# A two-layer decode kernel on Trainium2: four V pages loaded in five parts each, with uneven rows

## The chip, the cores and the metric

The kernel runs on one core of one Trainium2 chip. The metric is device microseconds for one execution; a profiled execution gives the trace that the views come from, and its own time stands beside its span.

## What is computed

One token goes through two layers with the same weights. Each layer adds attention over a sliding window of cached keys and values, and then a gated feed-forward block, each behind a layer norm:

```python
D, Hq, Hkv, Sk, Dh = 640, 32, 32, 32768, 192
W = min(4096, max(256, Sk // 4))                  # 4096
q = (x @ wq).reshape(B, Sq, Hq, Dh).transpose(0, 2, 1, 3)
k, v = k_cache[:, :, Sk - W:, :], v_cache[:, :, Sk - W:, :]
scores = einsum("bhqd,bhkd->bhqk", q, k) * (Dh ** -0.5)
o = einsum("bhqk,bhkd->bhqd", softmax(scores), v)
A = o.transpose(0, 2, 1, 3).reshape(B, Sq, Hq * Dh) @ wo
B = (silu(x @ w1) * (x @ w3)) @ w2                # D to 1536 to D

x = x + A(layernorm(x));  x = x + B(layernorm(x))
x = x + A(layernorm(x));  x = x + B(layernorm(x))
```

Everything is bf16. A head's keys are 4096 x 192 values, 1.5 MB, and so are its values; 32 heads, two layers and the weights make some 220 MB that have to come from memory.

## The kernel before

**Pages.** A head's K or V in the window is a page: 128 partitions of 6144 values (12,288 bytes), row `p` holding 32 consecutive positions. An arena of 32 units (half a page each) holds pages and weights. Some K pages of layer 0 stay for layer 1 (`RETAIN`, line 34).

**The list of loads.** Before any work is issued, `loads` is filled for both layers in the order in which data will be wanted (lines 196 to 242): three pieces of wq; then for `i` from 0 to 37 the V page of head `i - 6` and the K page of head `i` (`LEAD` is 6; for the last four K pages the K page first); then wo and the feed-forward weights; then the same for layer 1. An entry is a key, a number of units and a list of parts; a part is an offset, a width and the source in memory. A page has one part.

**Issuing.** `refill` (line 258) takes loads from the front of the list as long as `place` finds room, and issues each part from SyncE (line 279). It is called at the start and by `done` (line 297) whenever a page has been used and its units come free. All these loads stand on SyncE's queue in the order of the list, so a load that has to wait holds up those behind it. Waits are put in by the framework: for the readers of what was in the units before, for the landing of an earlier load on the same completion counter, of which there are eight for SyncE's loads, and in the readers for the landing of each load that they read.

**Use.** `k_page` turns a K page on VectorE (line 401) and multiplies it with the query on TensorE into `s_ps`; `softmax_head` and `softmax_place` make the weights of four heads at a time; `v_page` (line 455) multiplies a V page with them into `o_ps`, sixteen matmuls of 128 x 384, each of which reads all 128 partitions. V of head `g` is used in the round of K of head `g + 6`. `wo_proj` and `ffn` follow, and their weights go through the same arena; layer 1 starts with ten half-page loads of wq.

The order of instructions on each engine is the order in which the program is written (`pin`).

Of the kernel before, what the change touches and what calls it, by code (L numbers as in the profile page):

```python
# [25 lines left out]
PGW = 6144  # L26
# [3 lines left out]
U = PGW // 2  # L30
# [8 lines left out]
MW = 2 * HB  # L39
PW = MW * HB  # L40
SPLIT = (("k", 12), ("v", 8), ("k", 13), ("v", 9), ("k", 15))
KW = 4 * HB
WH = 6 * KW + 32 - KW
KEEP = 2400
# [4 lines left out]
def _ap(t, p0, npart, off, dims):  # L49
    ps = t.ap[0][0]  # L50
    return bass.AP(t.tensor, t.offset + p0 * ps + off, [[ps, npart]] + [list(d) for d in dims])
# [3 lines left out]
def kernel(  # L55
# [13 lines left out]
    nc = tc.nc  # L69
# [12 lines left out]
    def pin(ins):  # L82
        tc.keep_in_program_order(ins)
        return ins

    def mm(*a, **k):
        return pin(nc.tensor.matmul(*a, **k))  # L87
# [58 lines left out]
    arena = arn.tile([P, NUNIT * U], BF16, name="arena")  # L146
# [7 lines left out]
    loads = []  # L154
# [9 lines left out]
    def head(layer, g):  # L164
        return HG * ORDER[layer][g // HG] + g % HG

    def k_head(layer, g):
        return HG * ORDER[1][0] + (0, 1, 2, 3, 6, 4, 5, 7)[g] if layer == 1 and g < HG else head(layer, g)

    def k_first(layer, i):  # L170
        return layer == 0 and H - HB <= i < H

    def wo_units(layer):
        if layer == 0:
            return [(("o", 0, 0), [(1, 0, 2880)]), (("o", 0, 1), [(1, 2880, 5760)]), (None, [(0, 0, 5120), (1, 6720, 7680)]),
                    (("o", 0, 2), [(1, 5760, 6720), (2, 0, 1920)]), (("o", 0, 3), [(2, 1920, 4800)]),
                    (("o", 0, 4), [(2, 4800, 7680)]), (("o", 0, 5), [(3, 0, 2880)]), (("o", 0, 6), [(3, 2880, 5760)]),
                    (("o", 0, 7), [(3, 5760, 7680)]), (None, [(0, 5120, 7680)])]
        return [(("o", 1, 0), [(0, 0, 7680)]), (("o", 1, 1), [(1, 0, 7680)]), (("o", 1, 2), [(2, 0, 6720)])]
# [4 lines left out]
    def q_pieces(layer):  # L184
        if layer == 0:
            at = (0, 12, 24, 60)
            return [tuple(range(a, b)) for a, b in zip(at, at[1:])]
        return [tuple(range(12 * c + 6 * f, 12 * c + 6 * f + 6)) for f in range(2) for c in range(NCH)]

    def tail_cuts(width):  # L190
        return (0, width - TAIL), (width - TAIL, 640), (width - 1280, 1280)

    def units_of(width):
        return -(-width // U)

    for layer in range(2):
        for piece in q_pieces(layer):
            n, at = 512 * len(piece), 512 * piece[0]
            loads.append((("q", layer, piece[0]), units_of(n), [(0, n, wq_r[:, at:at + n])]))
        for i in range(H + LEAD):  # L200
            kinds = (("v", i - LEAD, A_v_cache), ("k", i, A_k_cache))
            for kind, g, cache in kinds[::-1] if k_first(layer, i) else kinds:
                if not 0 <= g < H:
                    continue
                h = k_head(layer, g) if kind == "k" else head(layer, g)
                if kind == "k" and layer == 1 and h in RETAIN:
                    if h == STASH:
                        loads.append((("k", 1, h), 2, []))
                    continue
                src = cache[0, h, S0:SK, :].rearrange("(p t) d -> p (t d)", p=P)  # L210
                if layer == 1 and (kind, h) in SPLIT:
                    for th in range(2):
                        loads.append(((kind, layer, h, th), 1, [(0, U, src[:, U * th:U * th + U])]))
                else:
                    loads.append(((kind, layer, h), 2, [(0, PGW, src)]))
        for key, ranges in wo_units(layer):
            at, parts = 0, []
            for pos, lo, hi in ranges:
                parts.append((at, hi - lo, wo_v[ORDER[layer][pos]][:, lo:hi]))
                at += hi - lo  # L220
            if key:
                loads.append((key, units_of(at), parts))
            else:
                dst = wo5 if at == 2560 else wo4
                if dst is wo5:
                    src = parts[0][2]
                    parts = [(o, n, src[:, o:o + n]) for o, n in tail_cuts(2560)]
                loads.append((None, None if dst is wo5 else LAST, [(dst[:, o:o + n], src) for o, n, src in parts]))
        if layer == 0:
            loads.append((("fa", layer), 1, [(0, 3072, w1_v[:, 0:3072])]))  # L230
            loads.append((("fb", layer), 1, [(0, 3072, w1_v[:, 3072:6144])]))
            loads.append((("fc", layer), 1, [(0, 1536, w1_v[:, 6144:]), (1536, 1536, w3_v[:, 0:1536])]))
            loads.append((("fd", layer), 1, [(0, 3072, w3_v[:, 1536:4608])]))
            loads.append((("fe", layer), 1, [(0, 3072, w3_v[:, 4608:])]))
            loads.append((("fg", layer), 1, [(0, W2A, w2_v[:, 0:W2A])]))
            loads.append((("fh", layer), 1, [(0, 7680 - KEEP - W2A, w2_v[:, W2A:7680 - KEEP])]))
            loads.append((None, None, [(keep[:, o:o + n], w2_v[:, 7680 - KEEP + o:7680 - KEEP + o + n])
                                       for o, n in tail_cuts(KEEP)]))
        else:
            loads.append((("fa", layer), units_of(7680), [(0, 7680, w1_v[:, 0:7680])]))  # L240
            loads.append((("fb", layer), 2, [(0, 4608, w3_v[:, 0:4608])]))
            loads.append((("fc", layer), 1, [(0, 3072, w3_v[:, 4608:])]))
            loads.append((("fd", layer), 2, [(o, n, w2_v[:, o:o + n]) for o, n in ((0, 3200), (3200, 1280), (4480, 3200 - KEEP))]))

    def place(key, n):
        at = [s for s in free if all(s + i in free for i in range(n))]
        if n == 2:
            at = [s for s in at if s % 2 == 0] or at
        kind, layer, x = (key + (None,))[:3]
        if layer == 0 and kind == "k" and x in RETAIN and x != STASH:  # L250
            return min((s for s in at if s < LAST), default=None)
        if layer == 0 and kind == "o":
            at = [s for s in at if s < LAST]
        if n == 1:
            return min(at, key=lambda s: (s ^ 1) in free, default=None)
        return max(at, default=None)

    def refill():
        while loads:
            key, n, parts = loads[0]  # L260
            if key is None:
                if n is not None:
                    if n not in free or n + 1 not in free:
                        return
                    free.remove(n)
                    free.remove(n + 1)
                for dst, src in parts:
                    pin(nc.sync.dma_start(out=dst, in_=src))
                loads.pop(0)
                continue  # L270
            s = place(key, n)
            if s is None:
                return
            home[key] = list(range(s, s + n))
            for i in home[key]:
                free.remove(i)
            loads.pop(0)
            for off, w, src in parts:
                pin(nc.sync.dma_start(out=arena[:, s * U + off:s * U + off + w], in_=src))  # L279
            if not parts:  # L280
                stash(arena[:, s * U:s * U + PGW], False)

# [97 lines left out]
    def build_w(layer, b, first):  # L380
        engs = (nc.gpsimd, nc.scalar) + ((nc.vector, nc.vector) if first else (nc.gpsimd, nc.scalar))
        for a in range(4):
            dst = _ap(wst[:], 32 * a, 32, KW // 4 * a + HB - 1, [[WH - 1, HB], [KW, 6]])
            src = _ap(qt_sb[:], 0 if first else 32 * a, 32, 6 * HB * b, [[6, HB], [1, 6]])
# [18 lines left out]
    def k_page(layer, g, s_ps):  # L403
# [4 lines left out]
        for n in range(6):  # L408
            it = 5 - n
            be, par = divmod(it, 2)  # L410
            first = g % HB == 0 and n == 0
            w = 32 if first else KW
            for th in range(2):
                mm(s_ps[32 * th:32 * th + w, :], lhsT=wst[:, hl, KW * it:KW * it + w],
                   rhs=_ap(half(key, th), 0, P, 64 * be + par, [[192, 16], [2, 32]]),
# [7 lines left out]
    def softmax_head(b, s_ps):  # L423
# [7 lines left out]
        mb = _ap(m8[:], 0, 32, 0, [[0, 4], [1, HB]])  # L431
        pin(nc.vector.tensor_scalar_mul(out=tb[0:32, 0:KW].rearrange("p (a z) -> p a z", a=4), in0=mb, scalar1=-SCALE))
        pin(nc.scalar.mul(out=tb[32:64, 0:KW].rearrange("p (a z) -> p a z", a=4), in_=mb, mul=-SCALE))  # L433
        pin(nc.vector.transpose(nbt[:], tb[:]))  # L434
# [280 lines left out]
```

## Time and profile before

| | |
|---|---|
| median of 2 runs (526.09 and 526.28) | 526.18 us |
| the profiled execution, its own time | 526.2 us |
| its span, first to last instruction | 524.4 us |
| TensorE busy | 281.4 us (54%) |
| VectorE busy | 252.4 us (48%) |
| ScalarE and GpSimd busy | 68.4 and 19.3 us |
| loaded from memory | 219.74 MB, 419 GB/s over the span |
| a page from its issue to its landing, median | 29.2 us |

The page cuts the span into 40 slices of 13.1 us. Its DMA line is the mean busy share of the core's sixteen DMA engines in tenths, and the GB/s line is what they moved in each slice. A line of waits reads: engine and line that waited, for what, microseconds in total, times, longest. A line of a timeline or of the chain starts with the time from the span's start and the duration. "SPq" is SyncE's queue, which issues the loads; "PE" is TensorE, "DVE" VectorE, "ACT" ScalarE.

### The profile page before, as it was taken

How to read it: one execution, taken by the hardware profiler on the slowest of the kernel's cores; microseconds unless marked ns; L12 is line 12 of the kernel's file. 1: busy time of each engine (PE TensorE's matmuls, PEld its weight loads, DVE VectorE, ACT ScalarE, POOL GpSimd, SP SyncE). 2: the span in 40 equal slices, each digit the busy share in tenths (PEclk: the TensorE clock that was granted, in tenths of full speed). 3: DMA queues.
4: the chain of work that ended last, by engine and by line, in shares of the span. 5: the costliest groups of instructions: out<-in, count | busy, mean ns of one | idle time of the engine just before them, and what ended most of it. 6: DMA issues, size and time to landing. Idle time of an engine off the chain costs nothing.

```text
span 524.4 us, 6002 instructions
## 1 busy us (share of the span) xinstructions
PE 281.4 (54%) x2392; PEld 110.1 (21%) x2392; DVE 252.4 (48%) x369; ACT 68.4 (13%) x208; POOL 19.3 (4%) x88
## 2 busy tenths in 40 slices
PE   3325655462654544635555785574256564464565
PEld 1101221121222211212112232232113221121132
DVE  0079875556747476753001107431678565555101
ACT  1010220110202020202001022121201120112001
POOL 4000000000000000000000001000000000000100
PEclk9967776577666657666556579889666768577566
DMA  9999999999999999999999999999999999999995
GB/s 376 406 430 429 429 427 429 427 429 432 426 431 431 425 432 430 427 427 433 424 417 413 376 413 426 430 430 428 428 429 430 431 427 430 431 427 430 431 428 237
DMA packets 24083, 220.12 MB, mean 420 GB/s; under 512 B 2808, under 2 KB 3704, under 8 KB 8952
## 3 DMA queue, kind: packets, MB, share of 16 engines
q1 hardware_dynamic: 23912, 219.75, 99.2%
q8 instruction: 19, 0.31, 0.2%
q14 instruction: 8, 0.07, 0.0%
q10 hardware_dynamic: 144, 0.00, 0.0%
HBM read 219.74 MB, written 0.00 MB: 419 GB/s over the span
## 4 chain that ended last, share of the span: by engine, by line
DMA 89%; PE 7%; DVE 2%; ACT 1%; issue 0%; SPq 0%; DVEq 0%; ACTq 0%
DMA arena<-in_A_k_cache_dram 43%; DMA arena<-in_A_v_cache_dram 30%; DMA arena<-in_B_w_dram 7%; DMA arena<-in_A_wq_dram 6%; DMA arena<-in_A_wo_dram 3%; PE s_ps L87 2%; PE o_ps L87 2%; DVE arena L401 2%; PE y_ps L87 1%; PE pss L87 1%; PE q_ps L87 0%; PE u_ps L87 0%; PE g_ps L87 0%; ACT w L588 0%; SPq L279 0%
## 5 line engine op out<-in xcount | busy, mean ns | idle before, releaser
L87 PE MATMUL s_ps<-arena,wst 128*16 128x512 bf16 (+1 forms) x768 | 156.5, 524 | 158.5 <-DVE arena L401 85.4
L401 DVE STREAM_TRANSPOSE arena<-arena 128x1536 uint32<-128x1536 uint32 x100 | 171.3, 1754 | 74.7 <-DMA arena<-in_A_k_cache_dram 74.3
L87 PE MATMUL o_ps<-arena,ptm 128*8 128x384 bf16 (+1 forms) x1024 | 112.3, 428 | 29.1 <-DMA arena<-in_A_v_cache_dram 24.5
L87 PEld LDWEIGHTS <-wst 128*16 128x16 bf16 (+1 forms) x768 | 48.4, 108 | 248.1 <-issue 210.2
L87 PEld LDWEIGHTS <-ptm 128*8 128x8 bf16 (+1 forms) x1032 | 41.2, 100 | 70.9 <-issue 57.3
L433 ACT ACTIVATE nt<-m 32x16 f32<-32x16 f32 x16 | 3.4, 213 | 272.2 <-DVE m L430 272.2
L449 ACT COPY ptm<-w 32x64 bf16<-32x64 bf16 x80 | 23.6, 295 | 45.4 <-PE o_ps L87 43.3
L87 PE MATMUL q_ps<-arena,xs 128*32 128x512 bf16 x120 | 19.2, 583 | 13.1 <-DMA arena<-in_A_wq_dram 12.0
L478 DVE SCALAR_TENSOR_TENSOR w<-pss,sc,cb 64x192 bf16<-64x192 f32 x16 | 6.5, 409 | 40.9 <-PE pss L87 40.9
L385 POOL COPY wst<-qt_sb 32x24 bf16<-32x24 bf16 x30 | 8.4, 279 | 421.9 <-PE s_ps L87 307.7
L424 DVE TENSOR_REDUCE lt<-s_ps 64x1 f32<-64x512 f32 x16 | 10.9, 684 | 24.4 <-PE s_ps L87 24.0
L87 PE MATMUL y_ps<-arena,otd 128*1 128x320 bf16 x176 | 15.3, 437 | 10.2 <-DMA arena<-in_A_wo_dram 9.8
L439 DVE STREAM_TRANSPOSE w<-w 64x512 bf16<-64x512 bf16 x16 | 11.3, 705 | 14.4 <-ACT w L436 14.4
L327 DVE CAST w<-y_ps 128x320 bf16<-128x320 f32 x3 | 1.5, 492 | 28.5 <-PE y_ps L87 28.5
L87 PEld LDWEIGHTS <-xs 128*32 128x32 bf16 x200 | 7.6, 112 | 31.7 <-issue 27.4
L449 DVE COPY ptm<-w 32x64 bf16<-32x64 bf16 x48 | 10.0, 209 | 8.8 <-PE o_ps L87 7.7
L385 DVE COPY wst<-qt_sb 32x24 bf16<-32x24 bf16 x4 | 1.1, 275 | 25.9 <-ACT qt_sb L372 25.8
L472 ACT CAST w<-o_ps 128x384 bf16<-128x384 f32 x16 | 7.7, 478 | 32.4 <-PE o_ps L87 25.1
L436 ACT ACTIVATE w<-s_ps,nt 64x512 bf16<-64x512 f32 x16 | 10.9, 682 | 5.6 <-DVE nt L434 5.6
L87 PE MATMUL pss<-w,sel 128*64 128x192 bf16 x32 | 6.2, 281 | 8.3 <-ACT w L472 6.9
L87 PEld LDWEIGHTS <-otd 128*1 128x1 bf16 x186 | 5.7, 102 | 19.9 <-issue 15.5
L87 PE MATMUL pss<-xsq,sc 128*128 128x6 f32 x16 | 4.7, 369 | 8.3 <-ACT xsq L104 7.5
(84 smaller groups left out, 117.0 us busy)
## 6 DMA issues: line engine op xcount, KB each, us to landing
arena<-in_A_v_cache_dram SPq DMA_DIRECT2D x62, 1536.0 KB, 29.2
arena<-in_A_k_cache_dram SPq DMA_DIRECT2D x47, 1536.0 KB, 29.2
arena<-in_A_wq_dram SPq DMA_DIRECT2D x10, 768.0 KB, 7.4
arena<-in_A_wq_dram SPq DMA_DIRECT2D x1, 4608.0 KB, 20.0
arena<-in_A_k_cache_dram SPq DMA_DIRECT2D x6, 768.0 KB, 10.6
arena<-in_A_wo_dram SPq DMA_DIRECT2D x6, 720.0 KB, 8.7
arena<-in_B_w_dram SPq DMA_DIRECT2D x5, 768.0 KB, 8.5
arena<-in_A_wo_dram SPq DMA_DIRECT2D x2, 1920.0 KB, 30.0
```

Of the source, the lines that this page charges most:

```text
L87: return pin(nc.tensor.matmul(*a, **k))
L327: pin(nc.vector.tensor_copy(out=y_sb[:, 320:640], in_=y_ps[1][:, 0:320]))
L385: pin((engs[a].copy if engs[a] is nc.scalar else engs[a].tensor_copy)(out=dst, in_=src))
L401: pin(nc.vector.transpose(x, x))
L424: pin(nc.vector.reduce_max(out=t0[:, 0:1], in_=s_ps[0:64, :], axis=AX.X))
L433: pin(nc.scalar.mul(out=tb[32:64, 0:KW].rearrange("p (a z) -> p a z", a=4), in_=mb, mul=-SCALE))
L436: pin(nc.scalar.activation(out=e[:], in_=s_ps[0:64, :], func=ACTF.Exp, bias=nbt[:, 0:1], scale=SCALE, accum_out=l[0:64, b % 2:b % 2 + 1]))
L439: pin(nc.vector.transpose(et[:], e[:]))
L449: pin((eng.copy if eng is nc.scalar else eng.tensor_copy)(out=dst, in_=src))
L472: pin(nc.scalar.copy(out=o_sb[:, 0:384], in_=o_ps[:, 0:384]))
L478: pin(nc.vector.scalar_tensor_tensor(out=om, in0=ot_ps, scalar=rl[0:64, b % 2:b % 2 + 1], in1=mask[0:64].unsqueeze(2).broadcast_to([64, 16 ...
```

## The change

Four V pages of layer 0 are loaded in five parts. They are the pages at places 1, 6, 11 and 16 of the V order, and `UNEVEN` gives each a number `k`: 8, 12, 14 and 10. The parts, all with the full 12,288 bytes of each row:

- 64 rows: partitions 0, 2, 4, ...
- 32 rows: partitions 1, 5, 9, ...
- 16 rows: partitions 3, 11, 19, ...
- `k` rows: partitions 7, 15, 23, ... (every eighth)
- `16 - k` rows: the rest of every eighth partition, from `7 + 8 k` on

A part carries a function that picks its rows, and `refill` applies it to the destination and the source. Offsets in the arena, order of the list, users and everything else stay.

```diff
+UNEVEN = {1: 8, 6: 12, 11: 14, 16: 10}
...
+    def uneven(src, k):
+        if k is None:
+            return [(0, PGW, src)]
+
+        def take(first, step, n):
+            def rows(x):
+                ps = x.ap[0][0]
+                return bass.AP(x.tensor, x.offset + first * ps, [[step * ps, n], list(x.ap[1])])
+            return rows
+
+        picks = ((0, 2, 64), (1, 4, 32), (3, 8, 16), (7, 8, k), (7 + 8 * k, 8, 16 - k))
+        return [(0, PGW, src, take(*pick)) for pick in picks]
...
-                    loads.append(((kind, layer, h), 2, [(0, PGW, src)]))
+                    loads.append(((kind, layer, h), 2, uneven(src, UNEVEN.get(g) if layer == 0 and kind == "v" else None)))
...
-            for off, w, src in parts:
-                pin(nc.sync.dma_start(out=arena[:, s * U + off:s * U + off + w], in_=src))
+            for off, w, src, *rows in parts:
+                dst = arena[:, s * U + off:s * U + off + w]
+                if rows:
+                    dst, src = rows[0](dst), rows[0](src)
+                pin(nc.sync.dma_start(out=dst, in_=src))
```

## The prediction

> **What bounds the kernel now.** I read the page first: the line of the DMA share, the bytes per second, the queues, the chain that ended last.
>
> ```profile
> span 524.4 us, 6002 instructions
> ...
> PEclk9967776577666657666556579889666768577566
> DMA  9999999999999999999999999999999999999995
> GB/s 376 406 430 429 429 427 429 427 429 432 426 431 431 425 432 430 427 427 433 424 417 413 376 413 426 430 430 428 428 429 430 431 427 430 431 427 430 431 428 237
> ...
> q1 hardware_dynamic: 23912, 219.75, 99.2%
> q8 instruction: 19, 0.31, 0.2%
> ...
> DMA 89%; PE 7%; DVE 2%; ACT 1%; issue 0%; SPq 0%; DVEq 0%; ACTq 0%
> ```
>
> The sixteen DMA engines are busy from the first slice to the last but one, at about 430 GB/s, and 89% of the chain is transfers. 219.75 MB at 430 GB/s are 511 us of the 524.4. So only what slows the engines, idles them, or makes the slowest of them later can move the time. The one dip is at the border of the layers: slices 20 to 24 (424, 417, 413, 376, 413) lie 107 GB/s in all under 430, which is 107 / 430 x 13.11 us = 3.3 us of lost transfer.
>
> Then what SyncE, which issues every load, waits for:
>
> ```profile
> SPq L279 <- DMA arena<-in_A_v_cache_dram: 196.0, 60, 7.3
> SPq L279 <- DMA arena<-in_A_k_cache_dram: 135.9, 43, 3.8
> SPq L619 <- DVE w L617: 22.3, 1, 22.3
> SPq L279 <- PE o_ps L87: 20.9, 18, 3.6
> ```
>
> and its timeline early in layer 0, around the first V page that the change splits (the 25.26 line; the others are issued at 63.29, 99.80 and 136.43):
>
> ```profile
> 21.63 0.33 SPq L279 DMA_DIRECT2D arena<-in_A_k_cache_dram  x1
> 25.26 0.33 SPq L279 DMA_DIRECT2D arena<-in_A_v_cache_dram  x1
> 28.90 0.33 SPq L279 DMA_DIRECT2D arena<-in_A_k_cache_dram  x1
> ```
>
> A page is 1.57 MB, 3.66 us at 430 GB/s, and one is issued every 3.64 us; it lands 29.2 us later (the median of the page's DMA issues). 29.2 / 3.65 = 8: SyncE keeps eight loads in flight and issues the next when the oldest has landed. That is what its 332 us of waiting on landings are.
>
> Last, the chain at the border of the layers:
>
> ```profile
> 288.40 1.60 PE y_ps L87 x11
> 290.00 0.02 issue
> 290.02 6.91 DMA arena<-in_A_wq_dram
> 296.93 0.04 issue
> 296.97 1.05 PE q_ps L87 x5
> 298.02 0.02 issue
> 298.04 6.53 DMA arena<-in_A_wq_dram
> 304.57 0.04 issue
> ```
>
> Here loads wait for buffers that PE frees, and PE for loads that have landed. So a load counts here when its slowest engine has landed it. The trace records sixteen completions a load, one an engine (without the engine's number), and I read how far the last lags the first. For the K page that lands from 42.89 to 43.45 us it is 0.56 us. At 44.08 us one engine carries an instruction packet of 16 KB (0.96 us; the q8 line), and the next load's last completion lags 2.13 us, the others 0.57 as before. Such packets come some 30 us apart, each makes one engine about 1.5 us later, and it stays late. The w2 load that lands at 286.75 to 289.79 has seven completions within 0.45 us, eight from 1.11 to 1.47, and one at 3.04. By the load that completes the chain at 304.57 the lag is 1.26: the earlier engines have idled meanwhile. At the kernel's last weight load it is 3.20 us again (mean 1.3).
>
> **The change, part by part.** The sum is against the profiled execution: 526.2 us, of which 524.4 are span and 1.8 lie around it; the median of the runs is 526.18, so no shift between them.
>
> Sixteen more issues on SyncE. Each takes 0.328 us (the rows of line 279), 5.2 us in all, beside 332 us of waits for landings: hidden, cost 0. Behind a waiting part stand all later loads, for SyncE issues in order. Five of the eight loads in flight now make up one page, so the store shrinks from eight pages to the three after it plus what is left of the split one: 3.5 pages or more, 12.8 us. That cover would have to fall to the time from issue to landing with nothing in front, 1.0 to 1.6 us for the store of the output at the end, before engines idle. The parts land within one page time, five full pages are issued after them, and the next split page is ten loads later. Cost 0.
>
> Packets. The rows stay 12,288 bytes. The packet records show one engine's rows starting 456.5 ns apart and the 4-byte packet that closes a load taking 6 ns (8 x 456.5 + 6 = 3,658 ns a page). Four more closing packets a page, four pages: 16 x 6 = 0.1 us on every engine, on the path. Cost +0.1 us.
>
> PE. The first matmul of a split page must see five landings in place of one: 16 more waits at some 0.017 us (SyncE's EVENT_SEMAPHORE row), 0.3 us. Behind them queue that page's sixteen matmuls and the next K page's. PE is busy 54% and in the stretch from 20 to 160 us waits for K transposes (33.0 us), never for V pages: hidden. Without that cover it would be the 0.3 us.
>
> Rows an engine carries. 64, 32 and 16 rows can be shared as 4, 2 and 1 by sixteen engines; k and 16 - k rows cannot be shared evenly. One engine can get none, one or two of them: 7 to 9 rows a page for 8 now, and 4 rows more or fewer in the four pages, 4 x 456.5 = 1.83 us. The total stays. How loads of fewer than 128 rows are dealt out, no row shows, for before has none. What it is worth is set at the border: if the latest engine there (3.04) is relieved, the next at 1.47 becomes the last, a gain of at most 1.57 us; if it gets four rows more, a loss of 1.83. After the border the lags start afresh, and the shift is carried to the end. The trace does not say which engines are the late ones, so between -1.57 and +1.83 I take 0.
>
> [...]
>
> Where the rows are written. A full page runs at 456.5 ns a row on every engine whether they are in step (0.56 us) or 2 us apart, so in a full page no engine is in another's way. For rows on every second, fourth or eighth partition the bounds are: nothing, as in the full pages, the nearest rows; and above, each row taking double because two engines share a way into the memory, 4 x 3.66 = 14.6 us. I take nothing, since rows and packets are the same size as now.
>
> Sum: 526.2 + 0 + 0.1 + 0 + 0 + 0 = **526.3 us**.
>
> **Rivals.**
>
> Relief. The late engines are those that get fewer rows. For it: the lag at 289.79 is one engine's, and 1.57 us of it are there to be had; the 3.3 us lost at the border are mostly this. Against: four page times with no regard to which engine is hit later. 526.3 - 1.57 = 524.7 us.
>
> Burden. The same with the other sign: the engine at 3.04 gets rows. 526.3 + 1.83 = 528.1 us.
>
> Engines in each other's way (the other side). If the rows of a part are dealt out in runs, the write ways that one engine had to itself in a full page are shared by two, while others lie idle. The price is up to one page time a page: 526.3 + 14.6 = 540.9 us when all engines are in step. They are in step to 0.56 us when the first split page comes and one to six of them are 1 to 2 us off later, which softens it: half is 533.6. It decides for slower by 2% (10.5 us) from 72% of the doubling on. Against it: 430 GB/s whatever the lags, in full pages.
>
> [...]
>
> Parts that wait for one another. If a part had to wait for the landing of the one before it, the eight loads would run dry sixteen times, at some 2 us each: about 558 us. The partitions of the parts are disjoint, so I give it little.
>
> Nothing moves: if the engine goes by the partition that is written, every engine keeps 8 rows, and the time is the forecast's.
>
> **How the numbers follow.** Forecast (nothing moves, or what moves does not meet the late engines; 525.7 to 527): 0.32. Relief: 0.27. Burden: 0.13. Engines in each other's way: 0.25, of which 0.11 are above 536.7. Waiting parts: 0.02. Faster by over 2%, which would take nearly all of the 13 us that the span lies above 511: 0.01. A measurement of this kernel tells about 2% from no change. Within 2%: 0.32 + 0.27 + 0.13 + 0.14 = 0.86; slower 0.11 + 0.02 = 0.13; faster 0.01. Range: 524.5 to 535.0 leaves 0.03 below and 0.17 above. Without the contention the time lies in 524.5 to 528.5.
>
> **What would show it.** SyncE's issues of line 279 rise by 16 with 0.33 us each, and 29.2 us stays the median landing. The GB/s of the slices around 55, 93, 130 and 167 us stay at 425 to 430 (a dip to 215 to 350 there is the third rival; dips to nothing are the waiting parts). The spread of the completions after 170 us tells relief, burden or nothing: 1.8 us in before. The chain at the border shows whether its landings at 296.93 and 304.57 come earlier or later. Wrong would be a loss outside these places, above all idle PE time in front of V pages.

## The result and the profile after

| | before | after |
|---|---|---|
| median | 526.18 us (526.09 to 526.28, 2 runs) | 570.92 us (570.32 to 571.52, 2 runs) |
| profiled execution, its own time | 526.2 us | 571.5 us |
| its span | 524.4 us | 569.4 us |

The ratio is 1.085 (95% interval 1.08 to 1.09): 44.7 us slower. The prediction was 526.3 us, with 524.5 to 535.0 as its range. Medians here and below are of runs in the usual, faster state; one run below, of e15_arena_runs, was in a slower one and is left aside.

First the page of the changed kernel; a slice is now 14.2 us. Line numbers of `k_turn` and `refill` have moved: 401 is now 418, and 279 is 296.

```profile
span 569.4 us, 6030 instructions
...
DMA  9999994599399489999899999999999999999996
GB/s 380 407 428 387 429 428 194 226 428 429 108 401 429 193 339 429 382 431 422 329 405 419 394 409 375 411 431 429 426 428 431 428 431 429 431 428 429 430 431 270
...
DMA 66%; PE 15%; DVE 9%; issue 6%; ACT 1%; SPq 1%; POOL 1%; DVEq 0%; POOLq 0%; ACTq 0%
```

The chain that ended last was 89% transfers and is now 66%; what has grown in it is PE (7% to 15%), VectorE (2% to 9%) and issue (0% to 6%). The GB/s line has three holes, near 85 to 114 us (194, 226), 142 to 157 (108) and 185 to 214 (193, 339). Taking each slice's lack against 430 GB/s times 14.2 us, the whole line lacks 57.5 us of transfer; the line of before lacks 12.4 us in the same way. The difference, 45.1 us, is the whole of the longer span. The three holes (to 171 us for the second) hold 14.6 + 11.7 + 10.8 = 37.1 us of it, the slice of 387 1.4, and the stretch from 270 to 370 us, around the layers' border, 8.9, where the border of before lacks 3.3.

Three stretches inside the holes, with the busy time of PE, PE's weight load, VectorE, ScalarE and GpSimd (their instructions in brackets), the clock, the DMA share and GB/s:

```profile
91.00:107.00 16.00, 4.62 (x20) 1.39 (x22) 10.50 (x13) 2.77 (x9) 0.55 (x2) 0.61 0.34 121
132.00:152.00 20.00, 3.21 (x12) 0.83 (x12) 4.06 (x5) 0.48 (x1) 0.00 (x0) 0.50 0.59 238
191.00:206.00 15.00, 6.38 (x56) 2.81 (x56) 11.53 (x12) 0.07 (x1) 0.56 (x2) 0.66 0.33 120
```

The DMA engines are idle for two thirds of the first and the third. So they are not slow here: nothing has been issued to them. The reason stands in VectorE's waits. The one row with a V page in it:

```profile
DVE arena L418 <- DMA arena<-in_A_v_cache_dram: 92.6, 4, 26.6
```

Line 418 is the transpose of K pages. It waits four times for a V page, 92.6 us in all, and there was no such row before. VectorE's timeline shows the four places (start, duration, and in the brackets the idle time ahead and its releaser):

```profile
57.16 3.44 DVE L418 STREAM_TRANSPOSE arena<-arena 128x1536 uint32<-128x1536 uint32 x2 [26.63 <-DMA arena<-in_A_v_cache_dram]
...
95.28 6.76 DVE L418 STREAM_TRANSPOSE arena<-arena 128x1536 uint32<-128x1536 uint32 x4 [23.83 <-DMA arena<-in_A_v_cache_dram]
...
145.89 3.44 DVE L418 STREAM_TRANSPOSE arena<-arena 128x1536 uint32<-128x1536 uint32 x2 [22.24 <-DMA arena<-in_A_v_cache_dram]
...
194.29 10.07 DVE L418 STREAM_TRANSPOSE arena<-arena 128x1536 uint32<-128x1536 uint32 x6 [19.94 <-DMA arena<-in_A_v_cache_dram]
```

In before the first of these transposes runs as soon as the query is ready:

```profile
29.70 3.44 DVE L401 STREAM_TRANSPOSE arena<-arena 128x1536 uint32<-128x1536 uint32 x2
```

The waits that the trace records with each instruction agree with that. The first K transpose of before waits on one landing counter. In the changed kernel it waits on five, those of the five parts of the V page at place 1, which it does not read; the transposes at 95.28, 145.89 and 194.29 us, which follow the issue of the pages at places 6, 11 and 16, wait on five, four and five, and so do the first K matmuls behind each. These waits are put in by the framework, which, by these waits, takes the two to overlap.

Now SyncE's timeline around the second split page (start, duration):

```profile
73.05 6.31 SPq L296 DMA_DIRECT2D arena<-in_A_v_cache_dram  x5
101.53 0.34 SPq L296 DMA_DIRECT2D arena<-in_A_k_cache_dram  x1
```

After the fifth part, at 79.4 us, SyncE issues nothing for 22 us. The next load needs units that K pages hold; their transposes wait for the V page just issued, so everything in flight has to land first, then VectorE and PE have to free a page. SyncE's waits name both, where before named mostly landings (196.0 and 135.9 us, and 20.9 for `o_ps`):

```profile
SPq L296 <- PE o_ps L88: 94.3, 35, 10.7
...
SPq L296 <- DVE arena L418: 70.0, 15, 19.4
SPq L296 <- PE s_ps L88: 51.0, 22, 6.4
```

### The profile page after: what moved, and what is told of

Read it like the earlier page. It is cut to its first block, busy times and chain, and to the rows that moved or that the text cites. A ratio compares the mean times of both kernels' runs of the same rounds, so it can differ in the third digit from the quotient of the medians.

```text
span 569.4 us, 6030 instructions
## 1 busy us (share of the span) xinstructions
PE 269.2 (47%) x2392; PEld 108.1 (19%) x2392; DVE 250.9 (44%) x369; ACT 68.3 (12%) x208; POOL 19.3 (3%) x88
## 4 chain that ended last, share of the span: by engine, by line
DMA 66%; PE 15%; DVE 9%; issue 6%; ACT 1%; SPq 1%; POOL 1%; DVEq 0%; POOLq 0%; ACTq 0%
DMA arena<-in_A_v_cache_dram 32%; DMA arena<-in_A_k_cache_dram 18%; PE s_ps L88 10%; DMA arena<-in_A_wo_dram 8%; DVE arena L418 7%; DMA arena<-in_B_w_dram 5%; PE o_ps L88 3%; DMA arena<-in_A_wq_dram 2%; SPq L296 1%; PE pss L88 1%; ACT ptm L466 1%; PE q_ps L88 1%; PE y_ps L88 1%; POOL wst L402 1%; DVE otd L499 0%
## 5 line engine op out<-in xcount | busy, mean ns | idle before, releaser
L88 PE MATMUL s_ps<-arena,wst 128*16 128x512 bf16 (+1 forms) x768 | 150.0, 503 | 224.3 <-DVE arena L418 162.6
L418 DVE STREAM_TRANSPOSE arena<-arena 128x1536 uint32<-128x1536 uint32 x100 | 170.0, 1748 | 124.8 <-DMA arena<-in_A_v_cache_dram 92.6
L88 PE MATMUL o_ps<-arena,ptm 128*8 128x384 bf16 (+1 forms) x1024 | 109.5, 413 | 15.6 <-DMA arena<-in_A_v_cache_dram 15.5
L402 ACT COPY wst<-qt_sb 32x24 bf16<-32x24 bf16 x30 | 8.7, 290 | 0.7
```

The costliest lines, as they stand in the source:

```text
L402: pin((engs[a].copy if engs[a] is nc.scalar else engs[a].tensor_copy)(out=dst, in_=src))
L418: pin(nc.vector.transpose(x, x))
```

## Experiments

The theory: the waits of the K transposes cost nearly all. The rival: the write side of the parts costs it (the prediction's third rival), and the waits only show where the time is lost. All kernels ran beside runs of before on the same chip.

| kernel | median, us (runs) | before there | ratio, 95% interval |
|---|---|---|---|
| e1_wait_only | 565.95 (2) | 525.6 | 1.077, 1.0741 to 1.0799 |
| e2_own_split | 534.05 (4) | 525.6 | 1.0169, 1.0142 to 1.0195 |
| e3_own_whole | 525.66 (10) | 525.6 | 1.0002, 0.9993 to 1.0012 |
| e4_own_even | 533.75 (4) | 525.6 | 1.0157, 1.014 to 1.0174 |
| e5_own_halves | 526.05 (10) | 525.97 | 1.0002, 0.9993 to 1.0012 |
| e6_src_plain | 533.29 (4) | 525.97 | 1.014, 1.0124 to 1.0155 |
| e7_dst_plain | 553.53 (4) | 525.97 | 1.0512, 1.048 to 1.0544 |
| e8_two_halves | 565.57 (2) | 525.97 | 1.0756, 1.0731 to 1.0781 |
| e10_page1 | 526.99 (10) | 525.85 | 1.003, 1.0019 to 1.0041 |
| e11_page6 | 538.89 (4) | 525.85 | 1.0254, 1.0237 to 1.0271 |
| e12_wait_late | 525.61 (10) | 525.85 | 1.0005, 0.9994 to 1.0016 |
| e13_thirtytwos | 525.62 (10) | 525.85 | 0.9999, 0.999 to 1.0009 |
| e14_half_ways | 543.2 (4) | 525.69 | 1.0314, 1.025 to 1.0377 |
| e15_arena_runs | 555.46 (3) | 525.69 | 1.0553, 1.0523 to 1.0583 |

### The wait alone, and the split alone

**e1_wait_only**: the kernel before, with the wait put in by hand.

```diff
+    OWN = [("v", 0, head(0, g)) for g in (1, 6, 11, 16)]
+    seen = []
...
+            if key in OWN:
+                seen.append(key)
             for off, w, src in parts:
...
         turned.add(key)
+        while seen:
+            pin(nc.vector.tensor_copy(out=pad[0:1, 0:1], in_=page(seen.pop())[0:1, 0:1]))
```

> The kernel before, its four V pages whole, and four VectorE copies of one element more: each reads one of the V pages 1, 6, 11 and 16, just before the K transposes that wait for the split pages in the changed kernel. Theory W (the time is lost because K transposes wait for V pages that are issued long before they are used): 560 to 575 us, with VectorE starting its first K transposes at 55 to 58 us instead of 29.7. Rival S (the time is lost in the split loads themselves, their rows or their number): 526 to 528 us, since here no load is split and four tiny copies cost under 0.5 us.

Measured: 565.95 us, 40.4 above before. Its page and its row of waits:

```profile
DMA  8999994799399399999899999999999999999996
GB/s 363 422 430 431 427 430 182 270 430 417 136 405 429 151 404 426 390 429 416 324 423 420 395 412 408 423 434 427 429 428 431 427 430 428 431 428 429 431 430 267
```

```profile
DVE pad L405 <- DMA arena<-in_A_v_cache_dram: 88.6, 4, 24.9
```

The pages are whole here, and the three holes are there all the same, in the same slices. The wait alone makes 40 of the 45 us.

**e2_own_split**: the change, but the four V pages go, one after the other, into a tile of their own (two units, taken from the arena), so that nothing else in the arena can be taken for them.

```diff
+    side = arn.tile([P, 2 * U], BF16, name="side")
-    arena = arn.tile([P, NUNIT * U], BF16, name="arena")
+    arena = arn.tile([P, (NUNIT - 2) * U], BF16, name="arena")
+
+    def span(s, off, w):
+        return side[:, s * U + off:s * U + off + w] if s < 2 else arena[:, (s - 2) * U + off:(s - 2) * U + off + w]
...
+        if key in OWN:
+            OWN.remove(key) if 0 in at and n == 2 else None
+            return 0 if 0 in at else None
+        if OWN:
+            at = [s for s in at if s >= 2]
...
-                dst = arena[:, s * U + off:s * U + off + w]
+                dst = span(s, off, w)
```

> The split of the changed kernel, part for part, but the four V pages go to a tile of their own (two units taken out of the arena), so that no K transpose and no K matmul waits for them. Theory W: most of the 44.7 us go; what stays is the stretched rows that the changed kernel's trace shows (12,288-byte packets of up to 900 to 1,100 ns for some 3 us around each split page, 1.3 to 2.3 us a page), so 531 to 536 us. Rival S: 560 us or more.

Measured: 534.05 us, 8.4 above before (7.5 to 10.2 by the interval). VectorE waits for no V page any more, and the engines never idle; but the slices of the split pages are thinner:

```profile
DMA  9999999999999999999999999999999999999995
GB/s 370 414 429 427 380 428 404 387 428 384 396 430 380 410 429 429 429 429 422 409 416 395 419 417 424 430 429 428 429 430 429 430 429 427 429 430 429 430 428 246
```

So there is a second, smaller cost, and it is one of busy engines. 40.4 + 8.4 are 48.8, 4 more than the change costs; some of the stretched transfer falls into time in which the engines would have run dry anyway. That last reading is inferred.

**e3_own_whole**: the same tile, with whole pages.

```diff
-UNEVEN = {1: 8, 6: 12, 11: 14, 16: 10}
+UNEVEN = {}
```

> As the run with the split pages in a tile of their own, but these pages come whole again, one load each: what the tile of its own costs by itself. Both theories: 526 to 527.5 us.

Measured: 525.66 us, no difference. The tile of its own costs nothing, so e2's 8.4 us are the split's.

**e4_own_even**: e2 with even parts.

```diff
-        picks = ((0, 2, 64), (1, 4, 32), (3, 8, 16), (7, 8, k), (7 + 8 * k, 8, 16 - k))
+        picks = ((0, 2, 64), (1, 4, 32), (3, 8, 16), (7, 8, 16))
```

> The tile of its own, with four parts of 64, 32, 16 and 16 rows: the same partitions, and no engine gets more rows than another. If uneven rows by themselves matter (an engine that gets up to four rows more or fewer), this lies 1 to 2 us off the run with k and 16 - k rows, to either side; if only the stretched rows of small parts matter, both agree within 1 us, at 531 to 536 us. Rival S in the form of too many parts: a fifth less of the loss than with five parts.

Measured: 533.75 us, against 534.05 with uneven parts, well within both intervals. That the rows are uneven, the subject of Relief, Burden and Nothing moves, costs nothing that can be measured.

### When the wait costs

**e8_two_halves**: the change in the arena, with two halves a page in place of five parts. Its parts are those of e5_own_halves (below), which has them in a tile of their own.

```diff
-        picks = ((0, 2, 64), (1, 4, 32), (3, 8, 16), (7, 8, k), (7 + 8 * k, 8, 16 - k))
+        picks = ((0, 2, 64), (1, 2, 64))
```

> The changed kernel with two parts in place of five, 64 rows on even and 64 on odd partitions, in the arena: no uneven rows and no small parts, but the same waits of K transposes and K matmuls for these pages. Theory W: 563 to 569 us, as the run that adds the wait alone to whole pages. Rival (small or uneven parts make the loss): 526 to 530 us.

Measured: 565.57 us, against 526.05 for the same loads in a tile of their own: 39.5 us. The row of waits:

```profile
DVE arena L418 <- DMA arena<-in_A_v_cache_dram: 87.3, 4, 25.5
```

Here the parts themselves cost nothing, and the wait costs its 40 us. It needs neither five parts nor uneven ones.

**e10_page1** and **e11_page6**: the change with one split page.

```diff
-UNEVEN = {1: 8, 6: 12, 11: 14, 16: 10}
+UNEVEN = {1: 8}
```

```diff
-UNEVEN = {1: 8, 6: 12, 11: 14, 16: 10}
+UNEVEN = {6: 12}
```

> The changed kernel with only the first of its four V pages split (k = 8); the other three come whole. Theory: the K transposes on VectorE and the K matmuls that follow the issue of a split page wait for all its parts to land. For the page at place 1 that puts the first transpose some 24 us later (29.7 to about 54 us), but the arena is filled far ahead, and eight loads are in flight; SyncE runs out of free units only some 27 us after the start of the stall, so the engines idle for a few us at most: 526 + 2 (stretch of the parts) + 0 to 3 = 528 to 531 us, and the GB/s stay above 380 in the slices after the first. Rival (each of the four waits costs alike, a quarter of the 44.7 us): 537 us, with a slice near 200 GB/s within 30 us after 54 us.

> The changed kernel with only the page at place 6 split (k = 12). Theory: compute runs close behind the loads at that time, so its stall of some 24 us leaves SyncE without free units for about 22 us and the engines idle for about 11.5 us (from the 16 us at 121 GB/s of the changed kernel's trace), 2 us of stretched parts besides, and a page or two of thinner transfer behind: 538 to 542 us; no idle time of VectorE in front of a K transpose at 54 us, one of 20 to 25 us near 95. Rival (a quarter of the loss for each page): 537, which the time alone does not tell from the theory; the trace does, for by the rival the GB/s would fall at once when the page is issued, and by the theory only some 20 us later.

Measured: 526.99 and 538.89 us, 1.1 and 13.0 above before. First page 1, VectorE's wait and the GB/s:

```profile
DVE arena L418 <- DMA arena<-in_A_v_cache_dram: 27.1, 1, 27.1
```

```profile
GB/s 373 408 432 427 383 426 429 430 430 426 432 430 425 432 432 423 431 430 429 427 408 416 412 420 426 432 428 426 431 430 428 430 429 429 431 428 430 429 426 234
```

VectorE stands still for 27.1 us, and the engines do not notice: only the slice of the split page itself is thin (383, 1.4 us). The expectation's 528 to 531 was too high: it allowed 2 us for the stretch and up to 3 for idling. SyncE still has free units to fill until 56.5 us, and the loads in flight by then last over the 8 us in which it waits for the next (to 64.8 us). Then page 6, VectorE's timeline and the GB/s:

```profile
92.80 6.75 DVE L418 STREAM_TRANSPOSE arena<-arena 128x1536 uint32<-128x1536 uint32 x4 [48.38 <-DMA arena<-in_A_v_cache_dram]
```

```profile
GB/s 367 418 428 428 432 429 313 124 417 429 426 429 430 428 430 430 427 431 427 429 420 420 412 423 425 433 423 431 431 426 430 430 427 431 430 425 433 427 430 225
```

The time is as expected, the stall is not: 48.4 us in place of 20 to 25, since without page 1's stall VectorE comes to the waiting transpose at 44.4 us, before the V page is even issued (63.2 us). The loss is no longer for it. The slices of 313 and 124 lack 13.2 us, and SyncE issues nothing from 78.4 to 99.0 us. So the length of VectorE's stall does not set the cost. What does is for how long the next load on SyncE needs units that are freed behind the stall: 8 us in e10, some 21 here.

**e12_wait_late**: the four one-element reads of e1, put where each page is used.

```diff
+                if layer == 0 and g in (1, 6, 11, 16):
+                    pin(nc.vector.tensor_copy(out=pad[0:1, 0:1], in_=page(("v", layer, head(layer, g)))[0:1, 0:1]))
                 v_page(layer, g, o_ps[b])
```

> The kernel before, all pages whole, and four one-element copies on VectorE that read the V pages at places 1, 6, 11 and 16, as in e1_wait_only, but each put in front of the sixteen matmuls that use the page, a page's turn after its load was issued six K pages earlier in the list. The copies write a scratch element that nothing uses, so nothing of the result is changed. Theory: what costs 40 us in e1_wait_only is that VectorE waits for a page that was issued up to the arena's whole depth ahead of the work; here the page has landed before the K page that VectorE turns next or lands just ahead of it, so 526 to 527 us and no wait for a V page above 4 us in VectorE's waits. Rival (a wait on a V page costs as such, or the four copies do): 535 us or more.

Measured: 525.61 us, no difference, and VectorE's waits name K pages alone:

```profile
DVE arena L401 <- DMA arena<-in_A_k_cache_dram: 71.0, 31, 7.7
```

The reads come when their pages have landed, so there is nothing to wait for, and four such copies cost nothing by themselves. In e1 and in the change VectorE gets to the wait some 22 us before the landing (88.6 and 92.6 us over four), and in front of work that frees the units for the next load.

**e15_arena_runs**: in the arena again, two parts on consecutive partitions.

```diff
-        picks = ((0, 2, 64), (1, 4, 32), (3, 8, 16), (7, 8, k), (7 + 8 * k, 8, 16 - k))
+        picks = ((0, 1, 64), (64, 1, 64))
```

> The changed kernel, in the arena, with two parts for each of the four V pages: partitions 0 to 63 and 64 to 127, not stepped. Theory: the waits of the K transposes come from the stepped partitions and not from the parts, so they are gone here (no V page in VectorE's waits), and the rows are stretched on the write side as in e7_dst_plain, 128 rows of each page at up to twice the time: 526 + 14.6 = 541 us, 536 to 550. Rival W (any page in parts brings the waits): 565 us or more, and a wait of some 25 us of VectorE for a V page near 54 us.

Measured: 555.46 us, 29.8 above before (27.5 to 30.6 by the interval), beyond the theory's 550 and short of the rival's 565. The wait for V pages is gone (the K row is the longest of VectorE's waits):

```profile
DVE arena L418 <- DMA arena<-in_A_k_cache_dram: 94.0, 33, 8.3
```

So the time alone was not decisive, and the waits are: it is the stepped partitions that bring them, not the parts. e5 has stepped partitions without the wait, in another tile; both are needed. Which comparison in the framework takes a stepped V page to overlap a K page, no run shows. With these waits gone and the DMA engines busy to the last slice but one, the 29.8 us are time of busy engines, which is the next subject.

### Where the rows are written

**e5_own_halves**: two halves of 64 rows in the tile of their own.

```diff
-        picks = ((0, 2, 64), (1, 4, 32), (3, 8, 16), (7, 8, 16))
+        picks = ((0, 2, 64), (1, 2, 64))
```

> The four V pages in a tile of their own, each as two loads: 64 rows on the even and 64 rows on the odd partitions. If the 8 us of the four-part split come from the small parts alone (in its trace the 64-row part lands 1.82 us after the page before it, the full rate, and only the 32- and 16-row parts are stretched): 525.5 to 527 us. If any part on stepped partitions is slowed, or every added load costs: 529 to 534 us.

Measured: 526.05 us, no difference. Parts as such, their closing packets and steps of two cost nothing that these runs can tell (0.08 us above before).

**e6_src_plain** and **e7_dst_plain**: e4's parts, stepped on one side only.

```diff
+        plain = ((0, 1, 64), (64, 1, 32), (96, 1, 16), (112, 1, 16))
-        return [(0, PGW, src, take(*pick)) for pick in picks]
+        return [(0, PGW, src, take(*pick), take(*row)) for pick, row in zip(picks, plain)]
...
-                    dst, src = rows[0](dst), rows[0](src)
+                    dst, src = rows[0](dst), rows[1](src)
```

That is e6; in e7 the last line has `rows[1](dst), rows[0](src)`.

> The four even parts (64, 32, 16, 16 rows) in the tile of their own, written to the same stepped partitions, but read from rows that follow one another in memory (0 to 63, 64 to 95, and so on), so the values of these pages land on the wrong partitions: that part of the computation is changed. Theory D (engines meet where they write): as the run with stepped reads, 533 to 535 us. Theory M (the stepped rows in memory slow the reads): 525.5 to 527 us.

> The other half: the four parts read the stepped rows of memory, but are written to partitions that follow one another (0 to 63, 64 to 95, 96 to 111, 112 to 127); the values land on the wrong partitions, so that part of the computation is changed. Theory M: 533 to 535 us, as with both stepped. [...]

Measured: 533.29 us for e6, as e4 with both sides stepped (533.75). 553.53 us for e7, 27.6 above before. Which rows are read makes no difference here. Which partitions are written does, and these consecutive ones cost more than e4's stepped ones (27.6 against 8.2 us).

**e13_thirtytwos** and **e14_half_ways**: three parts each, of 64, 32 and 32 rows, that differ only in the partitions of the last two.

```diff
-        picks = ((0, 2, 64), (1, 4, 32), (3, 8, 16), (7, 8, 16))
+        picks = ((0, 2, 64), (1, 4, 32), (3, 4, 32))
```

```diff
-        picks = ((0, 2, 64), (1, 4, 32), (3, 8, 16), (7, 8, 16))
+        picks = ((0, 2, 64), (1, 2, 32), (65, 2, 32))
```

> The four V pages in a tile of their own, as in e4_own_even, with parts of 64, 32 and 32 rows (every second partition, and twice every fourth) in place of 64, 32, 16 and 16. Theory A (rows of 32-row and 16-row parts alike take about twice as long): 64 rows of each page are stretched as in e4_own_even, so 533 to 535 us. Theory B (only the 16-row parts are stretched): as with two halves of 64, 525.5 to 526.5 us. Theory C (parts of 16 rows are stretched more than those of 32): between, 528 to 532.

> The four V pages in a tile of their own, parts of 64 rows (partitions 0, 2, 4, ...), 32 rows (1, 3, ..., 63) and 32 rows (65, 67, ..., 127). As many loads and rows a load as in e13_thirtytwos, which cost nothing; only the partitions of the two smaller parts differ. [...] Theory R (a part of one row an engine costs, whatever the partitions): 525.5 to 526.5. [...]

Measured: 525.62 and 543.2 us. The same number of rows on every fourth partition costs nothing, and on every second of one half costs 17.5 us (13.1 to 19.8 by the interval). First the GB/s of e13, then of e14:

```profile
GB/s 373 407 433 428 429 430 428 429 433 426 428 431 427 431 430 426 431 427 429 425 417 416 385 416 427 431 427 430 427 429 432 426 430 431 429 430 430 430 424 241
```

```profile
GB/s 362 422 431 400 385 430 352 371 429 356 370 430 355 370 431 428 428 431 378 368 401 381 414 386 418 429 427 431 429 428 426 434 429 427 430 431 427 431 428 248
```

e13's line is that of before. e14's has a pair of thin slices at each split page, with the engines busy. In the packet records of e13 a row takes 460 ns around the first split page (52 to 58 us). In those of e14 the median is 864 and 927 ns from 52 to 56 us, and in e15 914 to 956 from 50 to 56 us with 95% at or below 974: twice 460 is 920. So a row takes about twice as long there; why, no run shows. It is not the number of rows (32 in each of the two smaller parts of both kernels). In e4, then, the 32-row part was innocent, and the two 16-row parts on every eighth partition carry the 8 us. That their partitions make the difference, and not their number of rows, is told by e7, whose two 16-row parts go to sixteen neighbouring partitions each: there the rows that start from 55.5 to 57.5 us, shortly before these parts land, take 1,318 to 1,646 ns, about three times 460, where e4's rows around its 16-row parts take at most 1,014.

The size is another matter. By an estimate from the 0.457 us between the starts of two rows in before, plain doubling would add 4 x 32 / 16 x 0.457 = 3.7 us in e4 (measured 8.2), 7.3 in e14 (17.5) and 14.6 in e15 (29.8): what was measured is about twice that in each. The GB/s lines tell where the rest is. In e14 the slices of the first page lack 2.4 us, near the 1.8 of plain doubling; those of the other three lack 4.3, 4.2 and 4.3; and the slices from 245 to 326 us, around the layers' border, 7.9 against 3.4 in the same stretch of before. Why the later pages lack more than the first, no run shows. In before the engines are about as far out of step at each of the four: the last completion lags the first by 2.06 us in the V page that lands at 55.93 us, and by 1.89, 1.84 and 1.79 us in those that land at 92.47, 129.01 and 165.64 us.

## Why the prediction was wrong

**The bound**: right. The kernel is bound by the DMA engines at 430 GB/s, and the lack of transfer against 430 GB/s accounts for the loss to 0.1 us.

**SyncE's sixteen issues, 0 us**: their duration was right (0.33 us), and in e5 and e13 the added loads cost nothing (526.05 and 525.62 us). What failed is the step behind it, "five full pages are issued after them". For three of the four pages the next load could not be issued at all, because its units were not free while VectorE stood still. The store was reckoned in loads in flight alone, and not in free units.

**Packets, +0.1**: too small for these runs to tell from nothing; e5 is at 1.0002 (0.9993 to 1.0012). The trace of before gives such a packet 9 ns and not 6; sixteen of them are 0.1 us either way.

**PE: this is the step that failed.** The prediction wrote that "the first matmul of a split page must see five landings in place of one", priced the new waits at 0.3 us and called them hidden by a PE that "waits for K transposes (33.0 us), never for V pages". It took it that only the readers of a page wait for it. The runs showed four waits of 20 to 27 us on VectorE, in front of K transposes that read nothing of the page, worth 40.4 us by e1 and 39.5 by e8 against e5. The very cover it named, the K transposes, was what stopped. And the question that it asked of an added wait, who is queued behind it, was asked of PE and not of VectorE and SyncE. None of the rivals was this one: the waiting parts (558 us, 0.02) had SyncE wait, sixteen times, for 2 us.

**Rows an engine carries, 0 between -1.57 and +1.83**: right as far as it can be measured, since e2 and e4 agree (534.05 and 533.75 us). In the changed trace the loads of 8, 12, 14 and 10 rows have that many landings, and their counterparts 8, 4, 2 and 6, besides one early update 1.0 to 1.2 us after the issue, where loads of 64, 32 and 16 rows have sixteen. Which engines they are, no row shows. Relief and Burden were questions of 1.8 us in a case of 45.

**Where the rows are written, 0 between 0 and 14.6**: mis-sized. It is 8.4 us (e2). "Rows and packets are the same size as now" was no reason, because e6 and e7 have the same rows and packets and lie 20 us apart. The third rival had the write side and, at half, 7.3 us; rows that take twice as long stand in the records of e14 and e15 (medians of 864 to 956 ns against 460). That engines share a way into the memory, its reason for the doubling, no run shows. Its condition was too coarse, for it spoke of rows dealt out in runs, where in these runs it is the set of partitions of a part that counts, and of the change's parts only those on every eighth partition cost (e4, 8.2 us; e13, without them, nothing). Its softening by engines out of step is not seen: in e14 the later pages lack more than the first (4.2 to 4.3 us against 2.4), and in before the lag at the first of the four pages is 2.06 us already, and not the 0.56 that it reckoned with. So that its 533.6 us lies so near to e2's 534.05 is luck: plain doubling of the rows on every eighth partition is 3.7 us, and the runs do not show why they cost twice that.

**What would show it**: it named four places, at 55, 93, 130 and 167 us. The first has a dip, to 387, shallower than the 215 to 350 that were to be the third rival's. The holes lie at 91 to 107, 132 to 152 and 191 to 206 us, the first two near 93 and 130 us and the last 24 us behind 167, and by the prediction's own key a dip that deep would have been the waiting parts. Its sign of being wrong, idle PE time in front of V pages, did not come; VectorE idle in front of K pages did. The row that told the cause, VectorE's wait for a V page, was not among the signs.

So the sum by what was measured is 526.2 + 40.4 + 8.4 = 575.0 us (the 8.4 hold the packets), against 571.5 in the profiled execution; the 3.5 us between are put down to an overlap of the two terms, as inferred above.

## What to carry to other kernels

When an edit changes the form of an access (a step, a view, another shape) in a tile that many users share, look in the built program for who waits for whom before pricing anything: here the false waits, 92.6 us of VectorE's, stood in front of K transposes that share the tile, and not of the readers that the edit had in mind. Price a wait by what is queued behind it and by which buffers that work frees: here a stall of 27 us on VectorE cost about 1 us while units were free (e10), and one in front of a load that needed a unit cost 13 us (e11). And judge a small load by the set of partitions that it writes, not by its rows alone: here parts of 32 rows on every fourth partition cost nothing (e13, 525.62 us), and the same on every second of one half did cost (e14, 17.5 us).

## What the runs showed of the hardware

- A load's row of 12,288 bytes takes 460 ns in the packet records where the load's partitions are all 128, every second or every fourth (before, e13; the time of e5, 526.05 us, agrees). At the first split page it takes 864 to 956 ns, by medians of two microseconds, where they are 64 neighbours or every second of one half (e15, e14), and 1,318 to 1,646 ns where they are 16 neighbours (e7); every eighth costs too (e4, packet means of 623 and 625 ns from 52 to 56 us, in which full-rate rows are mixed).
- In three kernels the whole cost is about twice what the doubled rows themselves would make by the estimate above (8.2 against 3.7 us in e4, 17.5 against 7.3 in e14, 29.8 against 14.6 in e15); in e14 the excess lies at the later pages and at the layers' border.
- Reading every second, fourth or eighth row of memory in place of consecutive ones makes no difference that these runs can tell (e6 and e4, 533.29 and 533.75 us).
- VectorE stood still for 27 us in e10 at a cost of 1.1 us in all, the stretch of the parts included, while SyncE had units to fill and loads in flight.
